# Score blocks of two widths in one bank, and 64-row matmuls padded to 128 rows, in an attention and channel-mixing kernel

## The chip, the core and the metric

The kernel runs on one core of one Trainium2 chip. The metric is the device time of one execution in microseconds (us), as the median of several runs. A core has five engines with a queue each, which meet through semaphores: TensorE (PE; the loading of its stationary operand is listed apart, as PEld), VectorE (DVE), ScalarE (ACT), GpSimd (POOL) and SyncE (SP), which here issues the DMAs.

## The reference

Three stages follow one another. Sizes: 4 sequences of 576 positions, 8 heads of 64, so 512 features; 256 for the token mixing, 1536 and 1024 for the two hidden layers.

```python
# attention with a forget gate f
scores = q @ k.T / sqrt(64)
decay = cum[:, None] - cum[None, :]          # cum = cumsum(log(clip(f)))
attn = softmax(where(causal, scores + decay, -1e9))
x = attn @ v                                 # heads side by side: (4, 576, 512)
# token mixing and channel mixing
u = x + transpose(relu(transpose(x) @ w_tok1) @ w_tok2)
x2 = u + relu(u @ w_ch1) @ w_ch2
# gated layer
h = relu(x2 @ w_in)
out = (h * sigmoid(conv3(h))) @ w_out
```

Everything is float32 at the borders. Inside, most products are made of three passes over high and low parts.

## The kernel before, in words

**The order of the work.** `Order` (lines 20 to 144) is a planner. Every step is added with `T(engine, took, rank, fn, ...)`: its engine, a planned duration, a rank, what it reads and writes and which PSUM bank it takes. `run` then plays the steps through in these planned durations and always starts the step that can begin earliest; among those that could begin at the same time, the lowest rank goes first. The result is one fixed list for each engine. The rank does not hold a step back; it settles who goes first. `PER` (line 206) is the distance in rank from head to head: a pair of heads p has rank `t0 = 2 * p * PER`, and its scores, maxima, exponentials, transposes and value products get t0 plus small constants (lines 826 to 881). The ranks of weights and of the first part of the channel mix are also counted from multiples of PER (AVAIL and T_END, lines 994 and 1041), with constants that are not. The matmuls of the channel mix have LATE = 1000 added, so PE takes them when no head is ready.

**PSUM.** There are two rings (line 250): "z" with 2 buffers of two banks, [128, 2, 512] float32, for the scores, and "w" with 4 buffers of one bank for all else until the second stage.

**Heads.** 32 heads are worked in 16 pairs. The two heads of a pair lie on partitions 0 to 63 and 64 to 127, and with 64 rows each their matmuls run beside one another. The 576 query rows are cut in five blocks: block 0 has 64 rows, blocks 1 to 4 have 128, and block i attends to W[i] = 64 + 128 i keys. `score` (line 668) makes one block for both heads: products of queries and keys (line 688, float32, two records for each in the profile), and then a sum that adds the decay of the key (line 692: a selecting vector against the table `dec`). Block 4 is cut in two halves of 288 columns and takes a z buffer for each head; blocks 3, 2, 1 and 0 take a z buffer each, with one bank for each head. Block 0 uses only 64 query rows. `smax` (line 695) takes maxima on DVE and frees the bank, `sexp` (line 709) takes exponentials on ACT. Then probabilities are transposed: by PE for the first eight heads and the last two (line 745), by DMA for the others after a split in float16 parts by POOL and DVE (lines 721 and 727). `pv` (line 768) multiplies with the values, and `norm`, `xout`, `x_hi` and `x_lo` make x in a high and a low part; `x_lo` is a step on POOL.

**Token mixing.** Four heads make a group, and there are 8 groups. `t1` (line 884) multiplies x by w_tok1 in two halves, with the positions cut in five blocks of 64, 128, 128, 128, 128 rows: 15 matmuls a half (lines 234 to 236), three of them with 64 rows. `t2` (line 925) makes four outputs a group, for two blocks of features d and two halves of the positions e. Each begins with `t2_x` (line 915), which turns x by PE against an identity straight into the bank (line 921), and then come six matmuls with w_tok2. The half e = 0 turns blocks of 64, 128 and 96 rows, and e = 1 blocks of 32 (rows 96 to 127), 128 and 128.

**Channel mixing and the gated layer.** The first 3 of 12 blocks of the hidden layer (M1) are made while heads still run, in 8 chunks of 288 positions, with 36 + 36 matmuls each, as soon as a chunk's u is there. The other 9 blocks follow after the heads. Their weights (`weight`, line 270) are loaded in 64-bit words and unpacked by ACT, DVE, ACT and POOL (lines 297, 305 to 307, 223, 229), and their place is only free when the heads' pool "a2" is closed. After that come w_in, w_out and the gated layer.

**Set-up.** `dec` holds -8 times the running sum of log f in columns 0 to 575, made by ACT and DVE (lines 530 and 533), and once more its first 64 columns behind that (line 534).

Of the kernel before, what the change touches and what calls it, by code (L numbers as in the profile page):

```python
# [9 lines left out]
F32R = mybir.dt.float32r  # L10
# [3 lines left out]
AF = mybir.ActivationFunctionType  # L14
ALU = mybir.AluOpType
# [132 lines left out]
def fox_moe_kernel(  # L148
# [14 lines left out]
    nc = tc.nc  # L163
    NH, D, QKW = qk.shape
    B, S, H, _ = v.shape
# [9 lines left out]
    CH = S // 2  # L175
# [6 lines left out]
    W = [64 + 128 * i for i in range(NS)]  # L182
    Q0 = [0] + [64 + 128 * i for i in range(NS - 1)]
# [3 lines left out]
    ORDER = [4, 3, 2, 1, 0]  # L187
# [7 lines left out]
    PSC = 2.0 ** 15  # L195
# [7 lines left out]
    BY_PE = [n < 8 or n >= NH - 2 for n in range(NH)]  # L203

    FULL = 2 * HG
    PER = 7.0

    const = ctx.enter_context(tc.tile_pool(name="const", bufs=1))
    work = ctx.enter_context(tc.tile_pool(name="work", bufs=1))
# [9 lines left out]
    def f32(ap):  # L219
        return ap.bitcast(F32)  # L220
# [18 lines left out]
    pools = {}  # L239
# [12 lines left out]
    T = todo.add  # L252
    serial = [0]

    def turn(tag):

        serial[0] += 1
        return (tag, serial[0])

    def bank(tag):  # L260
        shape = [128, 2, 512] if tag == "z" else [128, 512]
        return psp.tile(shape, F32, tag=tag, name=tag, bufs=BANKS[tag])
# [215 lines left out]
    with tc.manual_schedule():  # L478

        ap1 = open_pool("a1", 1, "left")  # L480
# [6 lines left out]
        ident = ap1.tile([128, 128], F32, name="ident", bufs=1)  # L487
        ones = ap1.tile([128, 1], F32, name="ones", bufs=1)

        dec = ap1.tile([128, QKW - S], F32R, name="dec", bufs=1)  # L490
        sel = ap1.tile([128, NH], F32R, name="sel", bufs=1)

        nc.gpsimd.memset(mask[:, 0:128], 0.0)
# [27 lines left out]
        cum = ap1.tile([128, S], F32, tag="us", name="cum")  # L521
# [5 lines left out]
        for a in range(4):  # L527
            r = slice(NH * a, NH * a + NH)
            nc.vector.tensor_copy(sel[r], ident[r, NH * a:NH * a + NH])
        nc.scalar.activation(out=dec[:, 0:S], in_=cum, func=AF.Copy, scale=-8.0)  # L530
        for a in (1, 3):
            r = slice(NH * a, NH * a + NH)
            nc.vector.scalar_tensor_tensor(dec[r, 0:S], cum[r], -8.0, f32(dec[r, 0:S]), ALU.mult, ALU.subtract)
        nc.scalar.activation(out=dec[:, S:QKW - S], in_=f32(dec[:, 0:QKW - 2 * S]), func=AF.Copy)

        nc.gpsimd.memset(mask[:, 128:704], 0.0)
        nc.gpsimd.affine_select(
            out=mask[:, 512:640], in_=mask[:, 512:640], pattern=[[-1, 128]],
# [55 lines left out]
        def v_pow(g):  # L594
            sc = ap1.tile([128, 2], F32, tag="vsc", name="vsc", bufs=3)
            nc.vector.tensor_scalar(sc[:, 0:1], vps_t[g], 2.0 ** -86, None, ALU.max)
            si = sc[:, 0:1].bitcast(I32)
            nc.vector.tensor_scalar(si, si, 0x7F800000, 0x7F800000, ALU.bitwise_xor, ALU.bitwise_and)
            nc.vector.tensor_scalar(sc[:, 0:1], sc[:, 0:1], 8192.0, None, ALU.mult)
            nc.vector.tensor_scalar(sc[:, 1:2], sc[:, 0:1], PSC * 1e-9, None, ALU.mult)  # L600
            vs_t[g] = sc

        V_PARTS = ((slice(0, 64), slice(0, 1), slice(0, 1)),
# [40 lines left out]

        w1h = ap1.tile([128, NS, TOK], F32R, tag="w1h", name="w1h", bufs=1)
        w1l = ap1.tile([128, NS, TOK], F32R, tag="w1l", name="w1l", bufs=1)
        w2h = ap1.tile([128, KT, S], F32R, tag="w2h", name="w2h", bufs=1)
        w2l = ap1.tile([128, KT, S], F32R, tag="w2l", name="w2l", bufs=1)
        tok_w = [((w_tok1[0:64, :], [64, TOK]), w1h[0:64, 0, :], w1l[0:64, 0, :])]
# [13 lines left out]
        xf_t = {}  # L663
        z_t = {}
        pv_t = {}
        rs_t = {}

        def score(p, i):
            t = qk_t[p % QKB]
            w = W[i]  # L670
            rows = 64 if i == 0 else 128
            if i == 4:
                z = [bank("z") for _ in range(2)]
                hw = w // 2
                spans = [(S + 64 + e * hw, hw) for e in range(2)]
                out_ = [[z[x][:, e, 0:hw] for e in range(2)] for x in range(2)]
                for x in range(2):
                    z_t[2 * p + x, i] = z[x][:, :, 0:hw]
            else:
                z = bank("z")  # L680
                spans = [(S, w)]
                out_ = [[z[0:rows, x, 0:w]] for x in range(2)]
                for x in range(2):
                    z_t[2 * p + x, i] = z[0:rows, x, 0:w]
            halves = [slice(64 * x, 64 * x + 64) for x in range(2)]
            for e, (k0, n) in enumerate(spans):
                for x, r in enumerate(halves):
                    nc.tensor.matmul(out_[x][e], t[r, Q0[i]:Q0[i] + rows], t[r, k0:k0 + n], start=True, stop=False)  # L688
            for e, (k0, n) in enumerate(spans):
                for x, r in enumerate(halves):  # L690
                    h = 2 * p + x
                    nc.tensor.matmul(out_[x][e], sel[r, h:h + 1].to_broadcast([64, rows]), dec[r, k0 - S:k0 - S + n],  # L692
                                     start=False, stop=True)

        def smax(n, i):
# [122 lines left out]
        def x_lo(n):  # L818
            pool_sub(x_part(n, "xl"), x_of(n), f32(x_part(n, "xh")))

        PE_S = {4: 1.42, 3: 1.16, 2: 0.89, 1: 0.61, 0: 0.44}
        DVE_S = {4: 0.81, 3: 0.69, 2: 0.56, 1: 0.42, 0: 0.29}
        ACT_E = {4: 0.78, 3: 0.67, 2: 0.56, 1: 0.46, 0: 0.34}
        SEG = ((4, 3), (2, 1, 0))
# [1 line left out]
        def pair(p):  # L826
            t0 = 2 * p * PER
            kq = ("qk", p % QKB)
            A2, A3, A1 = ["a2"], ["a2", "a3"], ["a1"]
            if p:  # L830
                T("SP", 0.4, t0 - 9, load_qk, p, writes=[kq], moved=2.6, pools=A2)
            for i in ORDER:
                kz = [turn("z") for _ in range(2 if i == 4 else 1)]
                T("PE", PE_S[i], t0 + 1, score, p, i, reads=[kq], writes=[*kz, ("scores",)], pools=A2 + A1, ring=kz)
                for x in range(2):
                    n = 2 * p + x
                    kt = ("t", n % TB)
                    rank = t0 + x * PER
                    T("DVE", DVE_S[i], rank + 2, smax, n, i, reads=[kz[x % len(kz)]], writes=[(*kt, i), ("m", n % 3, i)],
                      pools=A2 + A1, ring=[kz[x % len(kz)]])  # L840
                    T("ACT", ACT_E[i], rank + 3, sexp, n, i, reads=[("m", n % 3, i)], writes=[(*kt, i)], pools=A2)
            for n in (2 * p, 2 * p + 1):
                rank = n * PER
                kt = ("t", n % TB)
                g = n // HG
                if BY_PE[n]:
                    for a, blks in enumerate(QUADS):
# [26 lines left out]
                for i in ORDER:  # L874
                    T("PE", (0.22 if n < FULL else 0.1) * len(PVB[i]), rank + 6, pv, n, i, reads=[*kp, *vk], writes=[kw, ("xf", g % 2, n % HG)],
                      pools=["a3"], ring=[kw])
# [4 lines left out]
                  writes=[("xl", n % HG)], pools=A1)  # L881


        def t1(g, a):
            st = tok[g]
            st["ps1", a] = bank("w")[:, 0:HG * D]
            c = slice(a * 128, (a + 1) * 128)
            terms = []
            for j in range(NS):
                r = slice(0, 64 if j == 0 else 128)  # L890
                terms.append((w1h[r, j, c], w1l[r, j, c], st["xh"][r, j, :], st["xl"][r, j, :]))
            mm3(st["ps1", a], terms)

        def t1_hi(g, a):
# [9 lines left out]
                st["t1l"][:, a, :], st["ps1", a], 0.0, f32(st["t1h"][:, a, :]), ALU.max, ALU.subtract)  # L904


        SEGS = [[], []]
        for j in range(NS):
            s0, n = (0, 64) if j == 0 else (64 + 128 * (j - 1), 128)
            for e in range(2):  # L910
                lo, hi = max(s0, e * CH), min(s0 + n, e * CH + CH)
                if lo < hi:
                    SEGS[e].append((j, n, lo - s0, hi - s0, lo - e * CH, hi - e * CH))

        def t2_x(g, d, e):

            st = tok[g]
            ps = bank("w")[:, 0:CH]
            c = slice(d * 128, (d + 1) * 128)
            for k, (j, n, a0, a1, b0, b1) in enumerate(SEGS[e]):  # L920
                nc.tensor.matmul(ps[:, b0:b1], xf_t[g][a0:a1, j, c], ident[a0:a1, a0:a1], is_transpose=True, start=(k == 0),  # L921
                                 stop=False)
            st["ps2", d, e] = ps

        def t2(g, d, e):
            t2_x(g, d, e)
# [72 lines left out]
        k = 0  # L999
# [8 lines left out]
        for g in range(NG):  # L1008
# [5 lines left out]
            if g % GB == GB - 1:  # L1014
                b = g // GB
# [26 lines left out]
        for k in range(M2):  # L1042
            m = M1 + k
            slots["ch1", m] = ("w2a", k)
            weight(col_block(w_ch1, m), big("p2a", "w2a", W2A, ("ch1", m), True), T_END + 2.4 * k, ("ch1", m),
                   reads=[("p2a",)], slot=[slots["ch1", m]])
        for k in range(M2):
            m = M1 + k
            slots["ch2", m] = ("w2b", k)
            weight(row_block(w_ch2, m), big("p2b", "w2b", M2, ("ch2", m), False), T_END + 20 + 2.4 * k, ("ch2", m),  # L1050
                   reads=[("p2b",)], pools_=["p2b"], slot=[slots["ch2", m]])
# [166 lines left out]
```

## Time and profile before

| | us |
|---|---|
| median of 3 runs | 781.96 |
| lowest and highest run | 779.5, 787.52 |
| the profiled execution | 782.84 |
| its span, first to last instruction | 781.0 |
| PE busy in it | 762.8 |
| DVE busy | 491.5 |
| POOL busy | 364.7 |
| ACT busy | 338.7 |

Durations come from the one profiled execution. Its span leaves out 1.84 us of its time. TensorE is pipelined: one record of a matmul may be three times as long as the distance to the start of the next, so the cost of a matmul in a row is read from start to start, and busy times of PE say how long anything was under way. The mean of the granted TensorE clock over the span is 0.983 of the full one.

### The profile page before, as it was taken

What the parts mean: (1) busy time and instruction counts of PE and PEld (TensorE: products, weight loads), DVE (VectorE), ACT (ScalarE), POOL (GpSimd) and SP (SyncE); (2) the same over time, 40 slices, a digit from 0 to 9 for tenths busy, and PEclk for the clock granted to TensorE, in tenths of its full rate; (3) what the DMA queues carried; (4) which work ended last, traced back from release to release, by engine and by line L of the source; (5) the groups of instructions that cost most, each with busy time, mean ns of one, the idle gap of its engine ahead of it and who ended that gap; (6) DMA issues with size and microseconds to landing.
All of it is one profiled execution on the core that took longest, in us unless ns stands there. A gap on an engine that the chain in (4) does not pass through costs nothing.

```text
span 781.0 us, 16260 instructions
## 1 busy us (share of the span) xinstructions
PE 762.8 (98%) x6428; PEld 714.1 (91%) x6428; DVE 491.5 (63%) x1075; ACT 338.7 (43%) x753; POOL 364.7 (47%) x448
## 2 busy tenths in 40 slices
PE   7999899999999999999999999999998999999997
PEld 5888788888888899999999999999998999999997
DVE  5687869777695667688731221124799866787651
ACT  5676545566465555653320220122453333233321
POOL 3253635784757335454521221223666655565441
PEclk6899889999999999999999999999999999999999
DMA  9344489899997906755442122124421110100000
GB/s 222 102 159 151 153 168 194 170 220 204 199 183 156 188 2 213 266 192 162 129 138 75 39 70 84 31 69 146 161 77 47 53 55 31 54 20 20 31 33 31
DMA packets 133453, 91.69 MB, mean 117 GB/s; under 512 B 86848, under 2 KB 125504, under 8 KB 133376
## 3 DMA queue, kind: packets, MB, share of 16 engines
q1 hardware_dynamic: 133376, 90.65, 45.1%
q8 instruction: 50, 0.82, 0.4%
q14 instruction: 27, 0.22, 0.1%
HBM read 53.01 MB, written 18.87 MB: 92 GB/s over the span
## 4 chain that ended last, share of the span: by engine, by line
PE 84%; DVE 10%; DMA 2%; ACT 1%; issue 1%; POOL 1%; SPq 0%; POOLq 0%; ACTq 0%; DVEq 0%
PE w L234 14%; PE w L235 13%; PE w L236 13%; PE z L235 8%; PE z L234 8%; PE z L236 8%; PE z L688 7%; PE w L777 3%; DVE cv L1119 3%; PE w L921 2%; PE z L692 2%; PE w L745 2%; DVE wexp L307 1%; PE w L782 1%; PE w L783 1%; PE w L784 1%
## 5 line engine op out<-in xcount | busy, mean ns | idle before, releaser
L234 PE MATMUL w<-uh,ww2a 128*128 128x288 f32 x352 | 104.3, 296 | 0.6 <-DVE r L425 0.5
L235 PE MATMUL w<-ul,ww2a 128*128 128x288 f32 x352 | 103.8, 295 | 0.0
L236 PE MATMUL w<-uh,ww2a 128*128 128x288 f32 x352 | 103.6, 294 | 0.0
L421 ACT ACTIVATE r<-w 128x288 fp32r<-128x288 f32 x96 | 39.0, 408 | 132.0 <-PE w L236 131.2
L712 ACT ACTIVATE t<-t,m 128x320 f32<-128x320 f32 (+4 forms) x160 | 82.5, 554 | 30.0 <-DVE m L706 27.1
L1119 DVE SCALAR_TENSOR_TENSOR cv<-hp,cw,cv 128x286 f32<-128x286 f32 (+1 forms) x128 | 89.1, 696 | 4.5
L234 PE MATMUL w<-uh,ww 128*128 128x288 f32 x288 | 86.8, 301 | 0.5 <-ACT hp L1112 0.5
L425 DVE SCALAR_TENSOR_TENSOR r<-w,r 128x288 fp32r<-128x288 f32 x96 | 42.9, 454 | 70.3 <-ACT r L421 70.0
L234 PE MATMUL z<-r,ww2b 128*128 128x288 f32 x288 | 85.0, 295 | 0.0
L235 PE MATMUL w<-ul,ww 128*128 128x288 f32 x288 | 85.0, 295 | 0.0
L706 DVE CUSTOM_DVE_ANT_0 t<-z,mask 128x320 f32<-128x320 f32 (+4 forms) x160 | 71.6, 482 | 21.3 <-PE z L692 20.6
L235 PE MATMUL z<-r,ww2b 128*128 128x288 f32 x288 | 84.8, 295 | 0.0
L236 PE MATMUL w<-uh,ww 128*128 128x288 f32 x288 | 84.7, 294 | 0.0
L236 PE MATMUL z<-r,ww2b 128*128 128x288 f32 x288 | 84.7, 294 | 0.0
L229 POOL TENSOR_TENSOR ul<-u,uh 128x288 fp32r<-128x288 f32 x64 | 57.9, 930 | 54.5 <-ACT uh L223 54.5
L234 PE MATMUL z<-g,ww2a 128*128 128x286 f32 (+1 forms) x256 | 76.1, 297 | 2.2 <-ACT o L223 1.0
L235 PE MATMUL z<-g,ww2a 128*128 128x286 f32 (+1 forms) x256 | 76.3, 298 | 1.6 <-POOL g L229 1.6
L236 PE MATMUL z<-g,ww2a 128*128 128x286 f32 (+1 forms) x256 | 75.4, 295 | 0.0
L688 PE MATMUL z<-qk 64*128 64x288 f32 (+4 forms) x384 | 67.6, 441 | 7.8 <-DVE m L706 5.6
L442 POOL TENSOR_TENSOR res<-res,u 128x288 f32<-128x288 f32 x32 | 26.2, 820 | 93.1 <-DVE res L439 85.9
L234 PEld LDWEIGHTS w<-uh,ww2a 128*128 128x128 f32 x352 | 66.0, 187 | 1.0 <-DVE r L425 1.0
L236 PEld LDWEIGHTS w<-uh,ww2a 128*128 128x128 f32 x352 | 66.3, 188 | 0.0
(136 smaller groups left out, 2187.4 us busy)
## 6 DMA issues: line engine op xcount, KB each, us to landing
wraw<-in_moe_w_ch_dram SPq DMA_DIRECT2D x24, 512.0 KB, 4.0
qk<-in_qk_dram SPq DMA_DIRECT2D x16, 608.0 KB, 4.4
u_d<-us SPq DMA_DIRECT2D x8, 576.0 KB, 4.4
p_d<-res SPq DMA_DIRECT2D x32, 144.0 KB, 3.1
u<-u_d SPq DMA_DIRECT2D x8, 576.0 KB, 5.0
res<-p_d SPq DMA_DIRECT2D x32, 144.0 KB, 2.6
x_d<-res SPq DMA_DIRECT2D x32, 144.0 KB, 1.8
u<-x_d SPq DMA_DIRECT2D x8, 576.0 KB, 4.1
```

What stands on the lines that cost most here:

```text
L229: nc.gpsimd.tensor_tensor(o, a, b, ALU.subtract)
L234: nc.tensor.matmul(ps, wh, xh, start=(first and i == 0), stop=False)
L235: nc.tensor.matmul(ps, wh, xl, start=False, stop=False)
L236: nc.tensor.matmul(ps, wl, xh, start=False, stop=(last and i == n - 1))
L421: nc.scalar.activation(out=t[:, 0, :], in_=box["z", m], func=AF.Relu)
L425: nc.vector.scalar_tensor_tensor(t[:, 1, :], box["z", m], 0.0, f32(t[:, 0, :]), ALU.max, ALU.subtract)
L442: nc.gpsimd.tensor_tensor(box["res", d], box["res", d], ubox["u"][:, d], ALU.add)
L688: nc.tensor.matmul(out_[x][e], t[r, Q0[i]:Q0[i] + rows], t[r, k0:k0 + n], start=True, stop=False)
L706: nc.vector.tensor_tensor_reduce(to, z_t.pop((n, i)), mk, -0.125, 3e38, ALU.add, ALU.min, m_t[n][0:rows, i:i + 1])
L712: nc.scalar.activation(out=tt[0:rows, o:o + w], in_=tt[0:rows, o:o + w], func=AF.Exp, bias=m_t[n][0:rows, i:i + 1], scale=-1.0)
L777: nc.tensor.matmul(o[:, 0:65], p32(n)[:, 128 * blk:128 * blk + 128], vp32_t[g][:, slot, hh, :], start=(j == 0), stop=(j == nb - 1))
L1119: nc.vector.scalar_tensor_tensor(cv, hp[:, s0 + t:s1 + t], cw[:, t, m:m + 1], cv, ALU.mult, ALU.add)
```

## The change

The score blocks 0 and 3 (64 + 448 columns) share a z buffer, and so do blocks 1 and 2 (192 + 320): each head's bank of 512 columns is then full. The products are still made block by block, the first with the flag that begins a bank; the decay of both blocks is added by one matmul of 512 columns for each head. Block 4 stays as it was. For this, `dec` becomes a table of 1216 columns in which each of the three sets finds its decay in one stretch; four copies on ACT make it instead of one. Block 0 is multiplied with 128 query rows instead of 64; its last 64 rows are not used. The planned costs of the three turns are 1.42, 1.33 and 1.28 in place of five. PER goes from 7 to 6. In a group of maxima and exponentials the order is now by head, then by block.

In `t1`, the first block is taken with 128 rows; rows 64 to 127 of w_tok1's parts are set to 0 by two memsets on POOL. In `t2_x`, each block is turned whole (128 rows, but 64 of the first block), into a bank of which the sum then uses the right 288 columns. The scale of the values' row sums gets a floor of 2^-125, so that rows without any keys stay finite.

```diff
-    PER = 7.0
+    PER = 6.0
...
-        dec = ap1.tile([128, QKW - S], F32R, name="dec", bufs=1)
+        DEC4, DEC12 = 128, S + 128
+        dec = ap1.tile([128, DEC12 + 512], F32R, name="dec", bufs=1)
+        dmain = dec[:, 64:64 + S]
...
-        nc.scalar.activation(out=dec[:, S:QKW - S], in_=f32(dec[:, 0:QKW - 2 * S]), func=AF.Copy)
+        for a, n in ((DEC12 - 64, 64), (0, 64), (DEC12, W[1]), (DEC12 + W[1], W[2])):
+            nc.scalar.activation(out=dec[:, a:a + n], in_=f32(dmain[:, 0:n]), func=AF.Copy)
...
-            nc.vector.tensor_scalar(sc[:, 1:2], sc[:, 0:1], PSC * 1e-9, None, ALU.mult)
+            nc.vector.tensor_scalar(sc[:, 1:2], sc[:, 0:1], PSC * 1e-9, 2.0 ** -125, ALU.mult, ALU.max)
...
+        nc.gpsimd.memset(f32(w1h[64:128, 0]), 0.0)
+        nc.gpsimd.memset(f32(w1l[64:128, 0]), 0.0)
...
-        def score(p, i):
+        SETS = {(4,): DEC4, (0, 3): 0, (1, 2): DEC12}
+        def score(p, blocks):
...
+                z = bank("z")
+                sums = [([z[:, x, :] for x in range(2)], d0, 512)]
+                products = []
+                at = 0
+                for i in blocks:
+                    products.append((i, [z[:, x, at:at + W[i]] for x in range(2)], S, W[i], at == 0))
+                    for x in range(2):
+                        z_t[2 * p + x, i] = z[0:64 if i == 0 else 128, x, at:at + W[i]]
+                    at += W[i]
+            for i, out_, k0, n, first in products:
                 for x, r in enumerate(halves):
-                    nc.tensor.matmul(out_[x][e], t[r, Q0[i]:Q0[i] + rows], t[r, k0:k0 + n], start=True, stop=False)
+                    nc.tensor.matmul(out_[x], t[r, Q0[i]:Q0[i] + 128], t[r, k0:k0 + n], start=first, stop=False)
...
-        PE_S = {4: 1.42, 3: 1.16, 2: 0.89, 1: 0.61, 0: 0.44}
+        PE_S = {(4,): 1.42, (0, 3): 1.33, (1, 2): 1.28}
...
-            for i in ORDER:
+            for blocks in SETS:
...
-                for x in range(2):
+                for x, i in ((x, i) for x in range(2) for i in blocks[::-1]):
...
-                r = slice(0, 64 if j == 0 else 128)
-                terms.append((w1h[r, j, c], w1l[r, j, c], st["xh"][r, j, :], st["xl"][r, j, :]))
+                terms.append((w1h[:, j, c], w1l[:, j, c], st["xh"][:, j, :], st["xl"][:, j, :]))
...
-            for k, (j, n, a0, a1, b0, b1) in enumerate(SEGS[e]):
-                nc.tensor.matmul(ps[:, b0:b1], xf_t[g][a0:a1, j, c], ident[a0:a1, a0:a1], is_transpose=True, start=(k == 0),
+            for k, (j, b) in enumerate(SEGS[e]):
+                n = 64 if j == 0 else 128
+                nc.tensor.matmul(ps[:, m + b:m + b + n], xf_t[g][0:n, j, c], ident[0:n, 0:n], is_transpose=True,
```

## Rows read from the trace of the kernel before

**Rows 1.** The page: busy time of PE, and the chain that ended last, by engine

```profile
PE 762.8 (98%) x6428; PEld 714.1 (91%) x6428; DVE 491.5 (63%) x1075; ACT 338.7 (43%) x753; POOL 364.7 (47%) x448
...
PE 84%; DVE 10%; DMA 2%; ACT 1%; issue 1%; POOL 1%; SPq 0%; POOLq 0%; ACTq 0%; DVEq 0%
```

**Rows 2.** Stages: window, length, busy PE PEld DVE ACT POOL, PEclk, DMA share, GB/s

```profile
107.00:284.00 177.00, 175.62 (x2074) 147.61 (x2072) 131.04 (x375) 102.66 (x225) 98.42 (x102) 1.00 0.88 179
...
333.00:377.00 44.00, 43.43 (x324) 42.81 (x323) 36.90 (x52) 20.28 (x43) 23.56 (x19) 1.00 0.58 182
...
86.00:104.00 18.00, 14.62 (x77) 11.94 (x77) 13.74 (x33) 6.49 (x15) 13.67 (x16) 0.72 0.54 151
```

**Rows 3.** The chain in order of time: start, duration, what

```profile
333.13 0.68 ACT wexp L297
...
376.83 0.40 PE w L234
```

**Rows 4.** Timeline of PE from 91 us: start, duration, what, idle before it

```profile
91.07 0.60 PE L688 MATMUL z<-qk 64*128 64x192 f32 x4 [2.50 <-DVE m L706]
...
93.27 0.58 PE L235 MATMUL w<-xl,w1h 64*128 64x256 f32 x1 [0.89 <-POOL xl L229]
...
100.65 0.93 PE L921 MATMUL w<-ident,xf 64*128 64x64 f32 x3
```

**Rows 5.** Timeline of PE, 201 to 208 us: turns of scores

```profile
201.12 1.02 PE L688 MATMUL z<-qk 64*128 64x448 f32 x4
...
202.27 0.20 PE L782 MATMUL w<-vp,pt 128*128 128x65 f16 x1
...
206.47 0.30 PE L235 MATMUL w<-ul,ww 128*128 128x288 f32 x1
206.60 0.29 PE L236 MATMUL w<-uh,ww 128*128 128x288 f32 x1
206.82 0.60 PE L688 MATMUL z<-qk 64*128 64x192 f32 x4
...
207.44 0.33 PE L688 MATMUL z<-qk 64*64 64x64 f32 x4
...
207.78 0.36 PE L234 MATMUL w<-xh,w1h 64*128 64x256 f32 x1
```

**Rows 6.** Timeline of PE, 213 to 217 us: block 4, then t2

```profile
213.48 1.24 PE L688 MATMUL z<-qk 64*128 64x288 f32 x8
...
214.83 0.56 PE L921 MATMUL w<-ident,xf 64*128 64x64 f32 x3
...
216.14 0.61 PE L921 MATMUL w<-ident,xf 64*128 64x64 f32 x3
216.54 0.38 PE L234 MATMUL w<-w2h,t1h 128*128 128x288 f32 x1
```

**Rows 7.** Groups by line and shape, weight loads of the products: busy, mean ns

```profile
L688 PEld LDWEIGHTS z<-qk 64*128 64x128 f32 x320 | 28.0, 195 | 20.4 <-DVE m L706 7.0 <-issue 4.8 <-DMA qk<-in_qk_dram 2.4
...
L688 PEld LDWEIGHTS z<-qk 64*64 64x64 f32 x64 | 3.2, 135 | 2.2 <-issue 0.8 <-DVE m L706 0.2
```

**Rows 8.** Timeline of PE, 209 to 212 us: second half of t1

```profile
209.59 0.28 PE L235 MATMUL w<-xl,w1h 128*128 128x256 f32 x1
209.71 0.28 PE L236 MATMUL w<-xh,w1l 128*128 128x256 f32 x1
209.92 0.38 PE L234 MATMUL w<-xh,w1h 64*128 64x256 f32 x1
...
212.00 0.20 PE L782 MATMUL w<-vp,pt 128*128 128x65 f16 x1
```

**Rows 9.** Timeline of PE, 57 us: transposes of 128 rows, then scores

```profile
57.20 0.71 PE L745 MATMUL w<-ident,t 128*128 128x128 f32 x5
57.84 1.24 PE L688 MATMUL z<-qk 64*128 64x288 f32 x8
```

**Rows 10.** Timeline of ACT at the start: the copy of line 534

```profile
9.91 0.26 ACT L534 ACTIVATE dec<-dec 128x64 fp32r<-128x64 f32 x1 [1.66 <-DVE dec L533]
```

More of the change, by code (lines that the diff above doesn't have):

```diff
@@ L529, in fox_moe_kernel @@
             nc.vector.tensor_copy(sel[r], ident[r, NH * a:NH * a + NH])
-        nc.scalar.activation(out=dec[:, 0:S], in_=cum, func=AF.Copy, scale=-8.0)
+        nc.scalar.activation(out=dmain, in_=cum, func=AF.Copy, scale=-8.0)
         for a in (1, 3):
             r = slice(NH * a, NH * a + NH)
-            nc.vector.scalar_tensor_tensor(dec[r, 0:S], cum[r], -8.0, f32(dec[r, 0:S]), ALU.mult, ALU.subtract)
-        nc.scalar.activation(out=dec[:, S:QKW - S], in_=f32(dec[:, 0:QKW - 2 * S]), func=AF.Copy)
+            nc.vector.scalar_tensor_tensor(dmain[r], cum[r], -8.0, f32(dmain[r]), ALU.mult, ALU.subtract)
+        for a, n in ((DEC12 - 64, 64), (0, 64), (DEC12, W[1]), (DEC12 + W[1], W[2])):
+            nc.scalar.activation(out=dec[:, a:a + n], in_=f32(dmain[:, 0:n]), func=AF.Copy)
         nc.gpsimd.memset(mask[:, 128:704], 0.0)
@@ L666, in fox_moe_kernel @@
         rs_t = {}
-        def score(p, i):
+        SETS = {(4,): DEC4, (0, 3): 0, (1, 2): DEC12}
+        def score(p, blocks):
             t = qk_t[p % QKB]
-            w = W[i]
-            rows = 64 if i == 0 else 128
-            if i == 4:
+            halves = [slice(64 * x, 64 * x + 64) for x in range(2)]
+            d0 = SETS[blocks]
+            if blocks == (4,):
                 z = [bank("z") for _ in range(2)]
-                hw = w // 2
-                spans = [(S + 64 + e * hw, hw) for e in range(2)]
-                out_ = [[z[x][:, e, 0:hw] for e in range(2)] for x in range(2)]
+                hw = W[4] // 2
+                sums = [([z[x][:, e, 0:hw] for x in range(2)], d0 + e * hw, hw) for e in range(2)]
+                products = [(4, out_, S + 64 + e * hw, hw, True) for e, (out_, _, _) in enumerate(sums)]
@@ L677, in score @@
                 for x in range(2):
-                    z_t[2 * p + x, i] = z[x][:, :, 0:hw]
+                    z_t[2 * p + x, 4] = z[x][:, :, 0:hw]
             else:
                 z = bank("z")
-                spans = [(S, w)]
-                out_ = [[z[0:rows, x, 0:w]] for x in range(2)]
-                for x in range(2):
-                    z_t[2 * p + x, i] = z[0:rows, x, 0:w]
-            halves = [slice(64 * x, 64 * x + 64) for x in range(2)]
-            for e, (k0, n) in enumerate(spans):
+                sums = [([z[:, x, :] for x in range(2)], d0, 512)]
@@ L689, in score @@
-            for e, (k0, n) in enumerate(spans):
+                    nc.tensor.matmul(out_[x], t[r, Q0[i]:Q0[i] + 128], t[r, k0:k0 + n], start=first, stop=False)
+            for out_, k0, n in sums:
                 for x, r in enumerate(halves):
                     h = 2 * p + x
-                    nc.tensor.matmul(out_[x][e], sel[r, h:h + 1].to_broadcast([64, rows]), dec[r, k0 - S:k0 - S + n],
+                    nc.tensor.matmul(out_[x], sel[r, h:h + 1].to_broadcast([64, 128]), dec[r, k0:k0 + n],
@@ L831, in pair @@
                 T("SP", 0.4, t0 - 9, load_qk, p, writes=[kq], moved=2.6, pools=A2)
-            for i in ORDER:
-                kz = [turn("z") for _ in range(2 if i == 4 else 1)]
-                T("PE", PE_S[i], t0 + 1, score, p, i, reads=[kq], writes=[*kz, ("scores",)], pools=A2 + A1, ring=kz)
-                for x in range(2):
+            for blocks in SETS:
+                kz = [turn("z") for _ in range(2 if blocks == (4,) else 1)]
+                T("PE", PE_S[blocks], t0 + 1, score, p, blocks, reads=[kq], writes=[*kz, ("scores",)], pools=A2 + A1,
+                  ring=kz)
+                for x, i in ((x, i) for x in range(2) for i in blocks[::-1]):
                     n = 2 * p + x
@@ L910, in fox_moe_kernel @@
             for e in range(2):
-                lo, hi = max(s0, e * CH), min(s0 + n, e * CH + CH)
-                if lo < hi:
-                    SEGS[e].append((j, n, lo - s0, hi - s0, lo - e * CH, hi - e * CH))
+                if max(s0, e * CH) < min(s0 + n, e * CH + CH):
+                    SEGS[e].append((j, s0 - e * CH))
+        MARGIN = [max(0, -min(b for _, b in seg)) for seg in SEGS]
         def t2_x(g, d, e):
             st = tok[g]
-            ps = bank("w")[:, 0:CH]
+            ps = bank("w")
             c = slice(d * 128, (d + 1) * 128)
-            for k, (j, n, a0, a1, b0, b1) in enumerate(SEGS[e]):
-                nc.tensor.matmul(ps[:, b0:b1], xf_t[g][a0:a1, j, c], ident[a0:a1, a0:a1], is_transpose=True, start=(k == 0),
-                                 stop=False)
-            st["ps2", d, e] = ps
+            m = MARGIN[e]
+            for k, (j, b) in enumerate(SEGS[e]):
+                n = 64 if j == 0 else 128
+                nc.tensor.matmul(ps[:, m + b:m + b + n], xf_t[g][0:n, j, c], ident[0:n, 0:n], is_transpose=True,
+                                 start=(k == 0), stop=False)
+            st["ps2", d, e] = ps[:, m:m + CH]
         def t2(g, d, e):
```

## The prediction

> **What bounds the kernel now.** First the page: TensorE is busy for 762.8 of 781.0 us and carries 84% of the chain that ended last [rows 1]. Busy time does not prove much for an engine whose records overlap, so the table by stages comes next [rows 2]. In the stage of the heads after the first ones (107 to 284 us) PE is busy 175.62 of 177.00 us at full clock (share 1.00, the 2.4 GHz level), DVE only 131.04; from 333 to 377 us PE is busy 43.43 of 44.00. So, after 107 us, what PE is given to do sets the pace, and a head that isn't ready is covered by matmuls of the first channel mix: 8 chunks x 72 of them by the code, 0.13 us each (206.47 to 206.60 [rows 5]). Third, the chain in order of time: from 333.13 us it leaves PE and runs through the unpacking of weights (ScalarE, VectorE, DMA) until PE takes over at 376.83 [rows 3], though PE lost only half a microsecond there. That stage is nearly balanced. Fourth, the timeline where PE does stop: at 91.07 after 2.50 us of waiting for VectorE's maxima, at 93.27 after 0.89 us for GpSimd's x low part [rows 4]; the clock of 86 to 104 us is 0.72 [rows 2], a mixture of its two levels. Before 107 us there is no channel mix to fill in, so there a chain through other engines can decide.
>
> The program order on each engine is fixed by the planner; in its own costs the scores get cheaper with the edit, the token mixing does not. So the durations below come from the trace, and the order can move a little.
>
> **Scores.** A turn is read from its first product's start to the start of whatever follows [rows 5]: block 3 (448 columns) 201.12 to 202.27 = 1.15 us, block 1 (192) 206.82 to 207.44 = 0.62, block 0 (64) 207.44 to 207.78 = 0.34. The difference of the first two over 256 columns is 2.07 ns a column; what is left is 0.62 - 192 x 0.0021 = 0.22 us a turn, whatever its width. Block 2 (320) comes to 0.88 that way. Four turns: 1.15 + 0.88 + 0.62 + 0.34 = 2.99 us a pair of heads. Afterwards there are two turns of 512 columns: 0.22 + 1.06 = 1.28 each, plus the price of a second set of products inside a turn. No row has unlike blocks in one turn. The nearest is block 4's turn, which has two sets of products and two of sums: 213.48 to 214.83 = 1.35 for 576 columns [rows 6], of which columns are 1.19, so its fixed part is 0.16 and the second set cost nothing. The other end is a whole fixed part, 0.22. I take 0 for (1, 2), as its products are as long as those of separate turns, and 0.10 for (0, 3): block 0's products stream 64 columns only, and their weight load grows from 64x64 to 64x128, mean 135 to 195 ns [rows 7], with too short a stream beside it to cover it. Two loads follow each other in a head's product, and the heads run side by side: some 0.1 us. So 2.66 instead of 2.99: 0.33 a pair.
>
> The rows on the loads are what the Trainium skill's page "TensorE: Matmul & The Clock Gate", section "LDWEIGHTS (loading the stationary operand)", leads one to expect: the time goes by columns loaded, not by rows contracted. It speaks against giving block 0 all 128 columns; as an estimate from its figure, 64 more columns in two loads would cost 0.11 us a pair, against 0 if the block-4 turn were the whole story. The trace (60 ns more per load) agrees with the page.
>
> A turn that follows a 128-row matmul also starts late: 206.60 to 206.82 is 0.22, where two 128-row matmuls stand 0.13 apart [rows 5]. Two turns fewer are up to 0.18 a pair; often turns are side by side already and save nothing. I take 0.10. Together 0.43 a pair, 16 pairs: **6.9 us**, between 0 (0.22 for both second sets, no entry saved) and 9.8 (0.43 + 0.18).
>
> The wider turns add two waits. The first maximum after (0, 3) waits for 1.38 us of PE work, not 1.15; ahead of it on VectorE stands the other head's block 4, planned at 0.81 in the code, so mostly hidden. And a score bank is now free only after four maxima. Behind it waits the next pair's block 4, which before, too, waited until everything was reduced; but (1, 2) itself no longer waits for the maxima of block 3, as block 1 did at 91.07 [rows 4].
>
> **Token mixing, first product.** With 64 rows, j = 0 pays on the way in and out: 209.71 to 209.92 is 0.21 where 209.59 to 209.71 is 0.12 [rows 8]. The half group from 209.92 to 212.00 takes 2.08; fifteen 128-row matmuls at 0.12 are 1.80. Saved: 0.28 within and 0.09 before it, less some 0.2 a group when it comes straight from scores (64 rows, so a switch stays). Two halves: 0.55 a group, 8 groups: **4.4 us**, between 2.9 and 5.9 (8 x 0.37, and 8 x 0.74). The same type and width on both sides makes this the surest term.
>
> **Token mixing, turned x.** For the second half of the positions, 32 + 128 + 128 rows take 216.14 to 216.54 = 0.40 [rows 6]. Five full turns in a row take 57.20 to 57.84 = 0.64 with the switch into scores (0.09) behind them [rows 9]: 0.11 each. Three become 0.11 + 0.11 + about 0.03, the last hidden under the next matmul: 0.25, and the switch before it (0.09) goes: 0.24 saved. The first half keeps its 64-row block and turns 32 columns more: 0.03 lost. Net 0.21 x 16 = 3.4 at best; if a full turn here costs nearer 0.17, 1.6; I take **2.6 us**, bounds -0.5 (nothing but the extra columns) and 4.
>
> **Set-up.** Four copies of the decay row on ScalarE instead of one of 0.26 us [rows 10]: about 1.1 us more before the first exponential, between 0 and 1.1 on PE's path. The two memsets of weight rows lie on GpSimd, which waits for weights then. Against it, the early pairs wait less for score banks, from nothing to about 2 us. I set the two off against each other. The floor in the scaling of v is a second operand of an existing instruction: 0.
>
> **What is not worth its full time.** Up to 93.27 us the first product of group 1 waits for GpSimd's low part, not for PE: pair 4's share, 0.4, is lost. And the pace: with PER = 6 and cheaper scores in the plan, heads are put closer, but if the plan has heads wait on VectorE, it moves channel mix matmuls forward instead, and the weights of the next stage (unpacked only after the heads' buffers close) then come no earlier. I deduct 1.5.
>
> Sum: 6.9 + 4.4 + 2.6 - 0.4 - 1.5 = 12.0 us. The profiled execution took 782.84 (span 781.0 and 1.84 around it), so 770.8; it lies 0.9 above the median of 781.96, which gives **770.0 us**.
>
> **Rivals.**
> *Absorbed at the weights (0.18).* The heads' end hardly moves; PE gets through its fill-in matmuls early, then waits where the chain already runs through weights [rows 3]. For it: that stage is balanced to 0.5 us. Against: before 333 us the chain is PE's, so unpacking shifts with PE if the order stays. Left are the gains before 107 us (5 pairs x 0.43 and two groups of about 0.85, less 0.4 = 3.5) and a share of the rest: 5 to 6 us, 776.5.
>
> *A further stall with a cold clock: slower (0.06).* One mechanism: between heads 4 and 12 nothing fills in, and denser ranks put eight maxima of a pair and weight unpacking in front of one another on VectorE, so both score banks stay taken and PE stops, as at 91.07. Its price from the present one: 2.50 + 0.89 of waiting, and then the first product of group 1, which takes 93.27 to 100.65 = 7.4 us [rows 4] where 207.78 to 212.00 is 4.2 [rows 5, 8]; with what follows until the clock is back, 8 us. One more leaves a gain of 4; from the second on it is slower: 786, with a third 794. Against: merged turns wait for fewer maxima.
>
> *The present stall goes too (0.10).* If denser ranks bring another pair's scores in front of group 1's first product, the 8 us vanish: 762.
>
> *The row count isn't the cause (0.04).* If the late starts belong to the kind of product and not to 64 rows, padding brings nothing: 6.9 - 1.9 = 5 us, 777. The pair 209.71 and 209.92 speaks against it.
>
> **Chances and range.** The forecast (764 to 774) has 0.62. Faster by over 1%, which is about what a measurement of this kernel can tell from no change: below 774.1, the forecast, the lost stall and a small part of the absorbed case, 0.76. Within 1% 0.18, slower by over 1% 0.06. The range runs from 758 (the stall gone and the upper bounds) to 782 (absorbed, with the lower bounds).
>
> **What would show it.** Scores: two turns of 512 columns a pair, of 1.38 and 1.28 us, and 128 records of the decay sums in place of 192. First product: 30 matmuls 0.12 apart, 3.7 us a group. Turned x: the second half at 0.25. PE busy in total down by 13 to 15 us, no new idle time. Wrong would be: turns near 1.5 us, a second stretch below full clock before 107 us, or PE idle between 300 and 377 us by several microseconds.

## The result, and the profile after

The changed kernel takes 769.8 us (median of 4 runs, 769.47 to 771.52), the kernel before beside it 782.32. The ratio is 0.9838, 95% interval 0.9808 to 0.9867: by that ratio 12.7 us less, with 10.4 to 15.0 inside the interval. The forecast was 770.0. The sum behind it was less good than that: two of its parts were wrong by some three microseconds each, in opposite directions.

The profiled execution took 771.52 us, span 769.7. The page's rows that answer to [rows 1]:

```profile
PE 745.4 (97%) x6364; PEld 707.8 (92%) x6364; DVE 495.1 (64%) x1075; ACT 337.4 (44%) x756; POOL 367.8 (48%) x450
...
PE 77%; DVE 9%; DMA 4%; POOL 4%; issue 3%; ACT 2%; SPq 0%; POOLq 0%; ACTq 0%; DVEq 0%
```

PE is busy 17.4 us less, but the span is only 11.3 us shorter: part of the saving has become idle time, and the chain runs on PE for 77% instead of 84%. The stages (answering to [rows 2], with the same columns) say where; the last two rows are one window in the kernel before and after:

```profile
107.00:284.00 177.00, 173.37 (x2047) 153.76 (x2046) 129.58 (x368) 106.19 (x239) 105.74 (x107) 0.99 0.85 175
86.00:104.00 18.00, 16.16 (x190) 13.90 (x186) 17.83 (x35) 8.06 (x18) 13.52 (x11) 1.00 0.80 185
320.00:374.00 54.00, 48.95 (x356) 47.09 (x354) 45.27 (x65) 23.16 (x47) 24.59 (x22) 1.00 0.53 169
...
270.00:400.00 130.00, 128.99 (x1094) 124.56 (x1093) 92.75 (x159) 64.08 (x144) 62.02 (x69) 1.00 0.53 164
270.00:400.00 130.00, 124.88 (x996) 122.23 (x995) 92.72 (x145) 60.97 (x132) 59.81 (x70) 1.00 0.53 165
```

From 107 to 284 us PE is idle for 3.6 us (1.4 before). From 320 to 374 us it is busy for 48.95 of 54.00, in the kernel before for 53.90; over 270 to 400 us it is idle for 5.1 us instead of 1.0. What PE waits for between 300 and 380 us (columns: engine, line, waited for; us in total, times, longest):

```profile
PE z L234 <- DVE res L439: 1.8, 2, 1.6
PE w L234 <- DVE r L425: 1.3, 1, 1.3
PE z L235 <- DVE r L425: 1.1, 1, 1.1
PE w L234 <- ACT res L223: 0.5, 1, 0.5
```

All but the last are VectorE's own small steps of the channel mix, in a queue between the steps that unpack weights. In the kernel before the same view has one row, 0.5 us. The prediction had named PE idle by several microseconds here as a sign of being wrong: the sign is there, with 4.7 us. The chain in order of time shows the stretch (answering to [rows 3]):

```profile
312.12 0.41 ACT r L421
...
374.00 0.40 PE z L234
```

It leaves PE at 312.12, some 21 us earlier than before (333.13), and comes back at 374.00, only 2.8 us earlier. And what was at 86 to 104 us has changed: the clock is 1.00 there, where it was 0.72. A smaller stop stands elsewhere:

```profile
160.19 0.38 PE L234 MATMUL w<-xh,w1h 128*128 128x256 f32 x1 [1.14 <-ACT xh L223]
```

PE waits there for the high part of x, then 0.59 us for the low part, and the granted clock is 0.50 from 161.4 to 164.7 us.

The terms of the sum are read from the timeline of PE, as before. Scores (answering to [rows 5]):

```profile
187.42 0.29 PE L236 MATMUL w<-uh,ww 128*128 128x288 f32 x1
187.64 1.25 PE L700 MATMUL z<-qk 64*128 64x64 f32 x8
...
188.94 1.03 PE L700 MATMUL z<-qk 64*128 64x192 f32 x8
...
190.15 0.20 PE L794 MATMUL w<-vp,pt 128*128 128x65 f16 x1
...
250.48 1.25 PE L700 MATMUL z<-qk 64*128 64x64 f32 x8
...
251.89 0.41 PE L234 MATMUL w<-uh,ww 128*128 128x288 f32 x1
...
255.28 1.13 PE L700 MATMUL z<-qk 64*128 64x192 f32 x8
...
256.58 0.38 PE L234 MATMUL w<-xh,w1h 128*128 128x256 f32 x1
```

A (0, 3) turn that stands alone takes 250.48 to 251.89 = 1.41 us (predicted 1.38), a (1, 2) turn alone 255.28 to 256.58 = 1.30 (predicted 1.28); where both turns stand side by side, they take 1.30 and 1.21, together 2.51 (predicted 2.66). That is the case in 8 of the 10 pairs that begin between 107 and 284 us.

First product of the token mixing and turned x (answering to [rows 8] and [rows 6]):

```profile
221.11 0.29 PE L236 MATMUL w<-uh,ww 128*128 128x288 f32 x1
221.25 0.49 PE L936 MATMUL w<-ident,xf 128*128 128x128 f32 x3
221.49 0.38 PE L234 MATMUL w<-w2h,t1h 128*128 128x288 f32 x1
...
224.72 0.28 PE L234 MATMUL w<-xh,w1h 128*128 128x256 f32 x1
...
228.31 0.20 PE L794 MATMUL w<-vp,pt 128*128 128x65 f16 x1
```

Thirty matmuls take 3.59 us instead of 4.22. Three whole turns take 0.24, and they start 0.14 after the matmul ahead of them.

### The profile page after: what moved, and what is told of

Same layout as the page of the kernel before. It is cut to its first block, busy times and chain, and to the rows that moved or that the text cites. A ratio compares the mean times of both kernels' runs of the same rounds, so it can differ in the third digit from the quotient of the medians.

```text
span 769.7 us, 16139 instructions
## 1 busy us (share of the span) xinstructions
PE 745.4 (97%) x6364; PEld 707.8 (92%) x6364; DVE 495.1 (64%) x1075; ACT 337.4 (44%) x756; POOL 367.8 (48%) x450
## 4 chain that ended last, share of the span: by engine, by line
PE 77%; DVE 9%; DMA 4%; POOL 4%; issue 3%; ACT 2%; SPq 0%; POOLq 0%; ACTq 0%; DVEq 0%
PE w L234 12%; PE w L235 12%; PE w L236 12%; PE z L234 8%; PE z L235 8%; PE z L236 8%; PE z L700 6%; PE w L789 4%; DVE cv L1134 3%; DMA wraw<-in_moe_w_in_dram 2%; PE w L936 2%; PE w L757 1%; DVE wexp L306 1%; PE z L704 1%; POOL ph L733 1%
## 5 line engine op out<-in xcount | busy, mean ns | idle before, releaser
L724 ACT ACTIVATE t<-t,m 128x448 f32<-128x448 f32 (+4 forms) x160 | 81.3, 554 | 22.2 <-DVE m L718 21.9
L234 PE MATMUL w<-uh,ww 128*128 128x288 f32 x288 | 86.3, 300 | 0.5 <-ACT hp L1127 0.5
L718 DVE CUSTOM_DVE_ANT_0 t<-z,mask 128x448 f32<-128x448 f32 (+4 forms) x160 | 70.0, 479 | 13.3 <-PE z L704 13.1
L235 PEld LDWEIGHTS w<-ul,ww2a 128*128 128x128 f32 x352 | 66.1, 188 | 0.0
```

The lines of the kernel that those rows point to most:

```text
L234: nc.tensor.matmul(ps, wh, xh, start=(first and i == 0), stop=False)
L235: nc.tensor.matmul(ps, wh, xl, start=False, stop=False)
L718: nc.vector.tensor_tensor_reduce(to, z_t.pop((n, i)), mk, -0.125, 3e38, ALU.add, ALU.min, m_t[n][0:rows, i:i + 1])
L724: nc.scalar.activation(out=tt[0:rows, o:o + w], in_=tt[0:rows, o:o + w], func=AF.Exp, bias=m_t[n][0:rows, i:i + 1], scale=-1.0)
```

## The experiments

**The parts one by one (e1, e2, e12, e3).** The padding of the first product alone:

```diff
-                r = slice(0, 64 if j == 0 else 128)
-                terms.append((w1h[r, j, c], w1l[r, j, c], st["xh"][r, j, :], st["xl"][r, j, :]))
+                terms.append((w1h[:, j, c], w1l[:, j, c], st["xh"][:, j, :], st["xl"][:, j, :]))
```

(with the two memsets and the floor of 2^-125, which stay in e3 too).

> The kernel before with the first product of the token mixing padded to 128 rows, and nothing else; the planned durations are the same, so the order of the work is too. If the step is worth its PE time: a group's 30 matmuls fall from 4.22 to about 3.7 us, 4.4 us in all (2.9 to 5.9), so 778 beside 782.3. If what PE saves before the second stage is absorbed by the wait for weights: the group at 3.7 us all the same, but 2 us or less in all, and PE idle for the rest between 320 and 380 us. If the late starts don't come from the 64 rows: groups stay at 4.2 us, no gain.

Measured: 776.84 us, ratio 0.9940 (0.992 to 0.996), 4.7 us less, 3.1 to 6.3. A group's 30 matmuls stand 0.12 apart. The group that begins straight behind scores, as the one of 4.22 us did, takes 3.69 here:

```profile
205.11 0.39 PE L234 MATMUL w<-xh,w1h 128*128 128x256 f32 x1
...
208.80 0.20 PE L784 MATMUL w<-vp,pt 128*128 128x65 f16 x1
```

The term is there, in full.

Turned x alone, `t2_x` and its list of segments as in the change:

```diff
-                nc.tensor.matmul(ps[:, b0:b1], xf_t[g][a0:a1, j, c], ident[a0:a1, a0:a1], is_transpose=True, start=(k == 0),
+                nc.tensor.matmul(ps[:, m + b:m + b + n], xf_t[g][0:n, j, c], ident[0:n, 0:n], is_transpose=True,
```

> The kernel before with x turned in whole blocks, and nothing else, in the same order of work. By PE time: the second half of the positions at 0.25 us instead of 0.40 and no late start, 2.6 us in all (1.6 to 3.4), so 779.7. Absorbed: 1 us or less. Nothing but more columns: 0.5 us slower.

Measured: 779.73 us, ratio 0.9978 (0.9963 to 0.9993), 1.7 us less. The interval, 0.5 to 2.9, holds the predicted 2.6 and part of the rival; alone it doesn't decide between them. So both paddings went in together:

```diff
+                terms.append((w1h[:, j, c], w1l[:, j, c], st["xh"][:, j, :], st["xl"][:, j, :]))
...
+                nc.tensor.matmul(ps[:, m + b:m + b + n], xf_t[g][0:n, j, c], ident[0:n, 0:n], is_transpose=True,
```

> The kernel before with both paddings of the token mixing and no other edit, in the same order of work. Alone they gave 0.9940 and 0.9978. If they add up as measured: 6.4 us less, 775.5. If both are worth their PE time (4.7 and 3.5 us): 8.2 us less, 773.7. If unpacking caps what can be had before the second stage: 5 us or less, 777 or more, with stops of PE between 330 and 380 us.

Measured: 775.61 us, ratio 0.9917 (0.989 to 0.9945), 6.5 us less, which is what the two gave one by one. The interval, 4.3 to 8.6, holds the 8.2 as well and just reaches the last case. Of the stops that the last case asked for, the trace has 2.7 us between 290 and 390.

The scores alone, at the old pace:

```diff
-            for i in ORDER:
+            for blocks in SETS:
...
     PER = 7.0
```

> The kernel before with the merged score turns (and their planned durations and table) alone, PER at 7, no padding. By PE time 6.9 us less (0 to 9.8), so 775.4; the turns at 1.38 and 1.28 us. If PER and the merging only work together, less than 3 us. The order of work changes a little, for a few us either way.

Measured: 778.14 us, ratio 0.9943 (0.9924 to 0.9962), 4.5 us less, 3.0 to 5.9: below the 6.9. The turns are as short as in the changed kernel; PE's waits between 300 and 390 us, 5.1 where the kernel before had 0.5, more than cover what is missing:

```profile
PE z L234 <- DVE res L439: 3.5, 3, 1.7
PE z L236 <- POOL ww2b L229: 0.8, 1, 0.8
PE z L235 <- DVE r L425: 0.5, 1, 0.5
PE z L234 <- ACT ww2b L223: 0.3, 1, 0.3
```

The three parts alone make 4.7 + 1.7 + 4.5 = 10.9 us. All three together at the same pace, PER = 7, are e4 below: 10.5 us. So they don't stand in each other's way by much.

**Is the rest lost to unpacking (e5, e6)?** In both kernels two of VectorE's three steps a block are left out for 26 blocks, the sign and the low bits of the weights of the second stage and the gated layer; the numbers are others, the loads and the planned order the same.

```diff
+            if not 13 <= r < 13 + 2 * M2 + KF:
-            nc.vector.scalar_tensor_tensor(c, box["raw"][0:p, 0:n, 1], -2 ** 31, c, ALU.bitwise_and, ALU.bitwise_or)
-            nc.vector.scalar_tensor_tensor(c, box["raw"][0:p, 0:n, 0], 29, c, ALU.logical_shift_right,
+                nc.vector.scalar_tensor_tensor(c, box["raw"][0:p, 0:n, 1], -2 ** 31, c, ALU.bitwise_and, ALU.bitwise_or)
+                nc.vector.scalar_tensor_tensor(c, box["raw"][0:p, 0:n, 0], 29, c, ALU.logical_shift_right,
```

> The changed kernel with less unpacking: of the weights of the second stage and the gated layer, the sign and the low three bits are left out (two of three steps on VectorE for 26 blocks), so the numbers are other ones; loads, order and planned durations stay. If the part of the saving that is missing waits for unpacking: PE's stops between 323 and 373 us go, and the time falls by 4 to 6 us, to 764 to 766. If it was lost to another order of PE's own work: 1 us or less, 769.

> The same left out of the kernel before. If unpacking was only just enough there, as the chain says (PE stopped 0.5 us): 0.5 to 2 us less, 780 to 781.5. If unpacking cost the kernel before as much as the changed one: 4 to 6 us less, and then it explains nothing of the difference.

Measured: the changed kernel falls to 761.64 us, ratio to the kernel before 0.9731 (0.9692 to 0.9769), which is 8 us less than with full unpacking; the kernel before falls to 779.06, ratio 0.9956 (0.9937 to 0.9975), 3.4 us less. Both gain more than expected, the changed one by far the more. With light unpacking the two kernels are 0.9956 - 0.9731 = 0.0225 apart, 17.6 us, against 12.7 with full unpacking. So some 5 us of what the change saves are taken back by the unpacking of weights. As a difference of two differences this has an uncertainty of about 4 us; the idle time of PE between 270 and 400 us agrees, with 4.1 us more in the changed kernel and at most 0.4 in either of the light ones.

**Transfers, or VectorE's steps (e7, e8, e9)?** A third buffer for raw weights in both kernels:

```diff
-                box["raw"] = work.tile([128, WSTN, 2], F32, tag="wraw", name="wraw", bufs=2)
+                box["raw"] = work.tile([128, WSTN, 2], F32, tag="wraw", name="wraw", bufs=3)
...
-        a, c = ("wraw", r % 2), ("wexp", r % 2)
+        a, c = ("wraw", r % 3), ("wexp", r % 2)
```

> The changed kernel with three buffers for raw weights instead of two, nothing left out. The chain of unpacking holds several transfers of 3 to 5 us that begin when a buffer comes free; with a third one they begin a block earlier. If those transfers hold up the stage: 2 to 4 us less, 766 to 768. If VectorE's three steps a block do (2.4 to 3.6 us with GpSimd beside them): within 1 us of 769.8.

> The kernel before with three buffers for raw weights. If its second stage is held by PE, as the prediction had it: within 1 us of 782.1. If by the transfers: 2 to 4 us less, as with the changed kernel.

Measured: 772.37 us (ratio to the kernel before 0.9862, 0.9824 to 0.9901) and 782.35 (0.9998, 0.9979 to 1.0017). Neither gains beyond the noise. Yet the transfers did hold up the unpacking: in e7 the first unpacking steps of the first and of the 24th block after the heads are 81.4 us apart, 92.9 in the changed kernel.

```profile
278.31 1.00 DVE L305 TENSOR_SCALAR wexp<-wexp 128x512 int32<-128x512 int32 x1 [0.44 <-ACT wexp L297]
...
359.67 0.41 DVE L305 TENSOR_SCALAR wexp<-wexp 128x512 int32<-128x512 int32 x1
```

VectorE is then busy for 78.6 of the 83 us from 277 to 360, and PE still idles 5.6 us between 270 and 400, where it idled 5.1. So weights that are ready earlier are not enough, as PE also waits for VectorE's own steps of the channel mix. (The third buffer changes the planned order too, in e8 so much that unpacking begins 4.6 us later than before; e8 alone proves little.) Then one VectorE step alone, the last of the three:

```diff
+            if not 13 <= r < 13 + 2 * M2 + KF:
-            nc.vector.scalar_tensor_tensor(c, box["raw"][0:p, 0:n, 0], 29, c, ALU.logical_shift_right,
+                nc.vector.scalar_tensor_tensor(c, box["raw"][0:p, 0:n, 0], 29, c, ALU.logical_shift_right,
```

> The changed kernel where only the last of VectorE's three unpacking steps is left out, for the weights of the second stage and the gated layer: these weights keep 20 of their bits behind the point instead of 23. If unpacking holds the second stage, one step of about 0.95 us in 26 blocks is enough to free most of it: 763 to 766. If it takes both steps to free it: 767 or more.

Measured: 761.06 us, ratio 0.9736 (0.9714 to 0.9759). One step is enough. This stage of the kernel now lies some 9 us earlier, and PE is busy in it all but 0.08 us (the row has the columns of [rows 2]); VectorE is busy for 30.78 us there, where the changed kernel had 45.27:

```profile
311.00:364.00 53.00, 52.92 (x399) 52.68 (x398) 30.78 (x54) 27.11 (x55) 32.73 (x28) 1.00 0.63 187
```

Where that stage begins and ends is seen from VectorE's first unpacking step, of the first and of the 24th block after the heads. Before:

```profile
288.46 0.58 DVE L305 TENSOR_SCALAR wexp<-wexp 128x512 int32<-128x512 int32 x1 [1.76 <-ACT wexp L297]
...
382.32 0.43 DVE L305 TENSOR_SCALAR wexp<-wexp 128x512 int32<-128x512 int32 x1
```

The changed kernel:

```profile
276.98 0.42 DVE L305 TENSOR_SCALAR wexp<-wexp 128x512 int32<-128x512 int32 x1
...
369.92 0.77 DVE L305 TENSOR_SCALAR wexp<-wexp 128x512 int32<-128x512 int32 x1 [1.75 <-ACT wexp L297]
```

The changed kernel without the third step (e9):

```profile
274.18 0.42 DVE L305 TENSOR_SCALAR wexp<-wexp 128x512 int32<-128x512 int32 x1
...
360.45 0.72 DVE L305 TENSOR_SCALAR wexp<-wexp 128x512 int32<-128x512 int32 x1 [2.06 <-ACT wexp L297]
```

From first to 24th block it is 93.9 us before, 92.9 after, and 86.3 with a step less. (That e9 begins 2.8 us earlier than the changed kernel is not its edit, which comes later; its heads had 6.8 us at the lower clock, the changed kernel's 13.7.) The change lets unpacking begin 11.5 us earlier and reach the 24th block 12.4 us earlier, and the profiled execution is 11.3 us shorter. This is no accident of one pair of traces: in e1, e2, e3, e4, e10, e11, e12 and the changed kernel, all with full unpacking and two buffers, the span moves by what the first of these steps moves, within 3 us. What counts of the savings, as far as these runs show, is how much earlier the heads let go of their buffers. The length of the unpacking alone does not tell the time, as e7 shows. This variant is as fast as the light one; it pays with precision, as those weights are cut to 20 bits behind the point.

**The pace (e4, e10, e11).** One line in each: the changed kernel at 7 and at 5, the kernel before at 6.

```diff
-    PER = 6.0
+    PER = 7.0
```

> The changed kernel with PER back at 7. If the pace of the heads matters little, as the prediction had it (nothing of its sum hangs on it): 768 to 772. If the denser pace brings the gain that the prediction put down to PE time: 774 or more. If it is the pace that starves the second stage of matmuls to fill in: 766 or less.

Measured: 770.54 us, ratio 0.9866 (0.9839 to 0.9894), against 0.9838 (0.9808 to 0.9867) at 6. The pace is worth nothing that can be told from noise here.

```diff
-    PER = 7.0
+    PER = 6.0
```

> The kernel before with PER at 6 and nothing else. If the pace is worth nothing by itself, as 770.5 against 769.8 for the changed kernel suggests: 780 to 784. If denser heads help or hurt where score turns are narrow: outside of that.

Measured: 791.97 us, ratio 1.0127 (1.0111 to 1.0143), 10 us slower. The first case failed, the second came true. The waits of PE between 60 and 200 us of e10:

```profile
PE z L688 <- DVE m L706: 6.7, 3, 3.2
PE w L235 <- POOL xl L229: 0.8, 1, 0.8
```

For the kernel before the first row reads 3.4 us in 2 waits. One of the new ones, in the timeline of e10:

```profile
168.43 1.34 PE L688 MATMUL z<-qk 64*128 64x320 f32 x4 [3.22 <-DVE m L706]
...
174.49 0.33 PE L688 MATMUL z<-qk 64*64 64x64 f32 x4 [1.65 <-DVE m L706]
```

Block 2 waits for maxima of the blocks before it, and the matmuls behind the first wait run at the lower clock (granted 0.50 from 168.6 to 171.9 us; value products are 0.05 us apart, 0.03 otherwise). The first unpacking step moves to 300.80, 12.3 us later than before. The waits are not all of that: PE idles 5.7 us between 107 and 270 us instead of 0.9, but the trace also has 378 matmuls of the channel mix ahead of this step, not 324, which at 0.13 us each is 7 us more. That is what the prediction feared of a denser pace, fill-in work moved in front of the heads. Behind it, between 270 and 400 us, PE idles 5.4 us instead of 1.0.

```diff
-    PER = 6.0
+    PER = 5.0
```

> The changed kernel with PER at 5. If the pace only shuffles the order: 768 to 773. If a denser pace moves channel mix matmuls out of the heads' stage and leaves them to cover the unpacking: 767 or less, with fewer stops of PE between 320 and 373 us.

Measured: 774.81 us, ratio 0.991 (0.9892 to 0.9927): 5 us slower than at 6. Neither expectation held; PE waits 6.5 us in 4 stretches for maxima in its trace, where the changed kernel at 6 has 1.2 us in 2.

## Why the prediction was right, and where it was not

**What bounds it.** Right for the heads: each part alone gave time, and in e1, e2 and e3 the first unpacking step behind the heads came 2.3 to 4.2 us earlier. Incomplete for the second stage. The prediction read "nearly balanced" from a half microsecond and still charged only 1.5 us, for the pace and for what comes next; e5 and e6 put it near 5. Together with 0.4 for pair 4, the deductions were 1.9. This is the term of the sum that was mis-sized most.

**Scores, 6.9.** Too small as PE time. Added up over the timeline from the first product of each stretch of scores to whatever follows, 11 pairs took 48.3 us between 105 and 280 us before, 10 pairs 39.7 after: 4.39 and 3.97 a pair, in 42 and 22 stretches. With 0.09 for each stretch that is gone (3.8 - 2.2 a pair) it is 0.42 + 0.14 = 0.56 a pair, 9.0 us in 16. The price of unlike blocks was right: (0, 3) takes 0.11 more than (1, 2) where each stands alone (1.41 and 1.30), predicted 0.10. What was missed is that two turns which need no maxima between them stand side by side in most pairs: the second saves 0.1 and both share one late start. That the extra 0.11 is the wider weight load was argued, not tested. In the run the merged turns gave 4.5 us alone (e3) and 4.0 on top of both paddings (e4 against e12, some 3 us either way), about half of their PE time.

**First product, 4.4.** Right: 4.22 to 3.59 is 0.63 a group, 5.0 us. The two groups are not entered alike; behind scores it is 4.22 to 3.69, and 8 groups at that are 4.2 us. e1 measured 4.7 (3.1 to 6.3). The rival that rows don't matter is out.

**Turned x, 2.6.** Right in size, with a slip in the reading: the row at 216.14 [rows 6] is a first half, it begins with 64 rows, so the 0.40 was not a second half. A second half in the kernel before is here:

```profile
180.36 0.29 PE L236 MATMUL w<-w2h,t1l 128*128 128x288 f32 x1
180.58 0.61 PE L921 MATMUL w<-ident,xf 32*128 32x32 f32 x3
180.95 0.38 PE L234 MATMUL w<-w2h,t1h 128*128 128x288 f32 x1
```

It takes 0.37, and 0.24 after; the start behind the last matmul falls from 0.22 to 0.14. That is 0.21 in 16 halves, 3.4 us of PE time; e2 and e12 found 1.7 and 1.8 of it in the run.

**The sum.** PE time of 9.0 + 5.0 + 3.4 = 17.4 us where the prediction had 13.9, and some 5 us given back where it had 1.9: 12.4 against 12.0. With light unpacking the two kernels are 17.6 us apart (14 to 21), which fits the PE time. So the forecast was hit with two errors of 3.5 and 3 us that cancelled; the mechanism was right, both sizes were off, and that the number came out within a microsecond is luck. A part of the gain may also be the clock: of 59 executions of the kernel before that ran beside the experiments, the 19 with a mean granted clock of 0.984 or 0.985 took 782.7 us in the mean, the 9 with 0.991 or 0.993 took 780.9. The changed kernel's four have 0.988 to 0.998, the kernel before 0.987 in the mean: as an estimate from these, 1 to 2 us of the 12.7.

**Set-up.** The copies take ScalarE 1.01 us instead of 0.26 [rows 10], so 0.75 more where about 1.1 was said, and the first exponential begins at 12.19 instead of 11.78:

```profile
9.86 1.01 ACT L538 ACTIVATE dec<-dec 128x64 fp32r<-128x64 f32 x4 [1.66 <-DVE dec L536]
```

**Rivals.** *Absorbed at the weights* came true by a third or so of the saving, not as a whole. *A further stall, slower* did not come at the size that was feared: the stop at 160.19 us costs the changed kernel 1.7 us of waiting and 3.3 us at the lower clock. e10 has waits for maxima of the feared kind in the kernel before at the denser pace, but they are only a part of its 10 us. That merging the turns is what makes PER = 6 harmless, since only block 4's maxima lie between a pair's three turns, is likely but not shown: the changed kernel also has both paddings, and no run has those alone at 6. *The present stall goes too*: in the profiled executions of the changed kernel and of e9, in the same order, the clock of 86 to 104 us is 1.00, and group 1's first product takes 3.8 us there (7.4 before). But its price was no fixed 8 us: in e1, e2 and e12, which keep the order of the kernel before, the clock of that window is 0.91, 0.91 and 0.81, against 0.72 [rows 2]. Its part in the gain stays open.

## What to carry to other kernels

When an engine sets the pace in one stage, price each saving in its own time, but ask of the stage behind it which other engine serves it there, when that engine can begin, and how much of its time is left. Here the time moved with the first step of unpacking, and some 5 us were lost behind it, where VectorE both unpacks weights and serves PE. Shortening the unpacking by a buffer brought nothing; taking work off VectorE brought 8 us. Pad short contractions to the full array where they stand in a stream of full ones: that pays at each change of the row count (0.09 us on the way in, about as much on the way out, in the rows of before). And put blocks in one turn where a bank has room: that saves the fixed part of a turn, 0.22 us here. Neither goes by the columns.

## What the runs showed of the hardware that was not expected

An unpacking step on VectorE lasts longer when it begins while GpSimd is at work. In the changed kernel, VectorE from 338 us:

```profile
338.43 0.69 DVE L306 SCALAR_TENSOR_TENSOR wexp<-wraw,wexp 128x512 int32<-128x512 int32 x1
339.16 0.69 DVE L307 SCALAR_TENSOR_TENSOR wexp<-wraw,wexp 128x512 int32<-128x512 int32 x1
...
340.87 1.53 DVE L305 TENSOR_SCALAR wexp<-wexp 128x512 int32<-128x512 int32 x1
```

and GpSimd:

```profile
340.82 1.29 POOL L229 TENSOR_TENSOR ww2b<-wexp,ww2b 128x512 fp32r<-128x512 f32 x1 [2.70 <-ACT ww2b L223]
```

The step of line 305 begins just after GpSimd's and ends at 342.40, 0.29 after GpSimd is done; alone, as at 276.98, it takes 0.42. So it is throughout. Of the 72 steps of 24 blocks in the changed kernel, the 31 that no GpSimd step touched took 0.41 to 0.43 (line 305) or 0.69 us (lines 306 and 307). All 32 that took longer began while a GpSimd step ran, and all but one of them ended 0.28 (line 305) or 0.55 us (lines 306 and 307) after it. The Trainium skill's page "SBUF — State Buffer", section "SBUF: two separate sides", says that the two engines share a pair of ports that one instruction holds to its end while the other blocks, if VectorE's instruction has two inputs in SBUF and GpSimd's reads SBUF, or if VectorE's is in a mode that uses two ports. Lines 306 and 307 have two such inputs, and these rows agree; line 305 has one, and no run here shows which mode it is in. Over the stage, by groups:

```profile
L306 DVE SCALAR_TENSOR_TENSOR wexp<-wraw,wexp 128x512 int32<-128x512 int32 x24 | 24.5, 1019 | 0.8
L307 DVE SCALAR_TENSOR_TENSOR wexp<-wraw,wexp 128x512 int32<-128x512 int32 x24 | 23.1, 963 | 0.8
L305 DVE TENSOR_SCALAR wexp<-wexp 128x512 int32<-128x512 int32 (+1 forms) x25 | 18.8, 751 | 15.1 <-ACT wexp L297 14.8
```

The three steps of a block mean 1.02 + 0.96 + 0.75 = 2.73 us where 0.69 + 0.69 + 0.42 = 1.80 is what they take alone: over 24 blocks, 22 us of the 93 go to waits for GpSimd's part. That is more than the 5 us which the change lost there. A kernel that moves those GpSimd steps elsewhere was not tried.
